# Linear attention and MLP on one Trainium2 core: the second product spread over two loops, token block 2 in row form, batch 0 read as loaded

## The chip, the core and the metric

The kernel runs on one core of a Trainium2 chip. TensorE (PE, with its weight loads listed as PEld), VectorE (DVE), ScalarE (ACT), GpSimd (POOL) and SyncE (SP) each work through their own instructions in order and wait for one another through semaphores; 16 DMA engines move data for the queues of POOL, SP and ACT. The metric is the device time of one execution in microseconds (us), the median of several.

## The reference

Eight batches, eight heads, 576 tokens, 64 features per head. Inputs and output are float32.

```python
kv  = einsum('bhsd,bhse->bhde', k, v)          # 64 x 64 per batch and head
o   = einsum('bhsd,bhde->bhse', q, kv)
rms = sqrt(mean(o*o, axis=-1) + 1e-6)
x   = (o / rms * g_norm) -> [4608 tokens, 512]  # heads side by side
h   = x @ w_in                                  # 512 -> 2048
g   = max(h, 0) + alpha * min(h, 0)             # alpha per feature
out = g @ w_out                                 # 2048 -> 512
```

## The kernel before

**Blocks.** The 4608 tokens are cut into nine blocks `w` of 512. A batch has 576 tokens, so a block holds tokens of one or two batches. All matmul operands are fp16; sums are fp32 in PSUM.

**Loads.** POOL's queue loads q, k and v of a batch and casts them to fp16. The first 512 tokens go into staging tiles (`qst`, `kst`, `vst`, L167), the last 64 into `qsb`, `ksb`, `vsb` (`load_rem`, L185). For batches 0 to 2 a partition holds several neighbouring tokens, so the output rows are stored in a permuted grid (`row_pieces`, L552). v is read by TensorE from where it was loaded. k, and q of the early batches, are first copied into an order by token (`regroup0` L215 for batch 0, `regroup` L191, in pairs on ACT from batch 3 on), and TensorE reads the copies.

**Attention in column form (blocks 0 to 2).** For each pair of heads `j`: `step_t` turns q with TensorE transposes (L327), and ACT or DVE copies the result to `qt_sb`; `step_kv` (L371) multiplies k by v for both heads at once, 128x128, and DVE keeps the two diagonal quarters by a mask (L379); `step_ot` (L393) gives o with features on partitions, 128x512; ACT squares it (L400), a matmul with a mask of ones adds the squares over the 64 features (`ssq_ps`, L416), ACT makes the reciprocal root (L420), and DVE writes `xt` (L429), the moving operand of the first product.

**Attention in row form (blocks 3 to 8, `W_ROW = 3`).** q is turned by DMA transposes on SP's queue (`dma_t`, L356). `row_kv` (L994) makes the 64x64 product of each head, and ACT copies them into `kv_masked`. `rows_mm` (L439) gives o with tokens on partitions, four tiles of 128 tokens. For each tile ACT squares 128x512 in one instruction (`rows_sq`, L463), DVE adds the squares with one reduction (`rows_ssq`, L469), ACT makes the reciprocal root of 128x8 (L479), DVE multiplies (`rows_norm`, L487), and a DMA transpose on SP's queue brings the tile into `xt` (L492).

**First product.** For each of 16 groups `g` of 128 of the 2048 features, four matmuls of 512 columns fill one PSUM bank (`m1_mm`, L507). ACT writes relu(-h) to `m_sb` (L514), and DVE writes `gt` = (1 - alpha) * relu(-h) + h (L518). From block 2 on two banks take turns for this (`h1`, `h2`; `h_bank`, L500), so group u + 2 can't begin before the `gt` of group u is written. From block 3 on the group at the head of a loop is split (`m1_cols`, L528): three quarters of its columns first, the last quarter after a few other matmuls, when the last tile of `xt` has come.

**Second product.** Block 0 uses 64 plain matmuls of 512 columns (`y_mm`, L539). Blocks 1 to 8 use a form with seven half-size products, 16 matmuls of 256 columns each (`prod_mm`, L656): products 1 and 2 read `gt` alone and collect in bank X, 6, 7 and 4 in bank Y, 5 and 3 in bank Z. Products 6, 5, 7 and 3 read sums of `gt` parts that DVE makes (`s_sum`, L616: S2, S1, S3, S4), and all but 1, 2 and 3 read sums of `w_out` parts made once (`w_sum`, L592). DVE and ACT read the banks between products (`y_read`, L713) and POOL, SP or ACT store the rows.

**Order.** It is written out by hand. The early part (L805 to L960) lists block 0 and the attention of block 1 step by step. Then loop `w` from 1 to 8 (L1056) has 16 units `u`. A unit holds one group of the first product of block `w`, then seven matmuls of the second product of block `w - 1` (`PER`, `Y_LIST`; none in loop 1, whose units hold the last three plain matmuls of block 0 instead), then steps of the attention of block `w + 1` (`attention`, L1032, with the tables `ATT_1` and `ROW_AT`). Loads of batch `w + 2` are issued at the head of loop `w` (`load_gated`, L204). After loop 8 comes the second product of block 8. `g_norm` is applied to `xt` for blocks 0 to 2 and folded into `w_in` during loop 2 (`scale_w_in` on ACT, L246).

Of the kernel before, what the change touches and what calls it, by code (L numbers as in the profile page):

```python
# [9 lines left out]
FP32 = mybir.dt.float32  # L10
# [7 lines left out]
def kernel(  # L18
# [32 lines left out]
    W_ROW = 3  # L51
# [81 lines left out]

    alpha_row = ysb_p.tile([P, D_MODEL], FP32, name="y_sb")
# [11 lines left out]
    for i in range(NBUF):  # L146
        t = {}
        for nm in ("k", "v", "q") if i < 2 else ("k", "v"):
            n = 1 if nm == "v" else T0 if i == 0 else NT
            t[nm] = qkv_p.tile([P, n, H, D], FP16, name=f"{nm}sb{i}")  # L150
            if i > 0 or nm == "v":
                nc.vector.memset(t[nm][REM:P, n - 1, :, :], 0.0)
        bufs.append(t)
    stages = {}

    def load0(nm, j, n=1):
        i, h = divmod(2 * j, HH)
        if (0, nm, i) not in stages:
            stages[0, nm, i] = stage_p.tile([P, HH, T0, D], FP16, name=f"{nm}st", tag=f"{nm}st")
# [5 lines left out]
    def load_main(b, nm, h0=0, h1=H):  # L165
        if (b, nm) not in stages:
            stages[b, nm] = stage_p.tile([P, H, TPP, D], FP16, name=f"{nm}st", tag=f"{nm}st")  # L167
# [5 lines left out]
    def load_q(b):  # L173
        st = stage_p.tile([P, TPP, H, D], FP16, name="qst", tag="qst")
# [7 lines left out]
    def buf_of(b, nm):  # L182
        return bufs[min(b, B_NAT) % 2 if nm == "q" else b % NBUF][nm]

    def load_rem(b, nm):  # L185
        nc.gpsimd.dma_start(
            out=buf_of(b, nm)[0:REM, 0 if nm == "v" else TPP, :, :],
# [16 lines left out]
    def load_gated(b):  # L204
        load_rem(b, "q")
        if b == B_NAT:
            load_q(b)
        load_rem(b, "k")
        load_main(b, "k")
        if b > B_NAT:  # L210
            load_q(b)
        load_rem(b, "v")
        load_main(b, "v")

# [6 lines left out]

    def regroup_pair(b, nm, j):
        regroup(b, nm, 2 * j, 2 * j + 2, nc.scalar)

# [17 lines left out]
    def scale_w_in(g):  # L242
        i = max(n for n, f0 in enumerate(IN_CUTS[:-1]) if f0 <= g * P)
        f0 = g * P - IN_CUTS[i]
        blk = w_in_sb[i][:, :, f0 : f0 + P]
        nc.scalar.activation(out=blk, in_=blk, func=AF.Copy, scale=g2col[:])  # L246

    def load_w_out(i):
        t = w_p.tile([P, GW, D_MODEL], FP16, name=f"w_out_sb{i}")
        for r in range(0, GW, GW // 2):  # L250
            g = i * GW + r
            nc.gpsimd.dma_start(
                out=t[:, r : r + GW // 2, :],
                in_=moe_w_out[g * P : (g + GW // 2) * P, :].rearrange("(g p) m -> p g m", p=P),
            )
        w_out_sb.append(t)
# [20 lines left out]
    for i in range(len(IN_CUTS) - 1):  # L277
        load_w_in(i)
    load_batch(1, ("k",))
    load_w_out(0)  # L280
    load_main(1, "q")
    load_w_out(1)
# [3 lines left out]
    load_w_out(2)  # L286
    load_w_out(3)
    load_rem(1, "q")

# [13 lines left out]
    kv_masked = [const_p.tile([P, NPAIR, P], FP16, name=f"kv_masked{i}") for i in range(2)]  # L303
# [20 lines left out]
    def transposes(qt_ps, c, b, j, ts):  # L324
        n = rows(b)
        for t in ts:
# [29 lines left out]
    def dma_t(b, ts=tuple(range(NT))):  # L356
        qt = qt_sb[b % 2][:, :, PAD : PAD + S]
        for t in ts:
            c0, c1 = t * P, min((t + 1) * P, S)
            src = stages[b, "q"][:, t] if t < TPP else buf_of(b, "q")[0:REM, TPP]  # L360
# [5 lines left out]

    def step_kv(b, j, pool=(ps_s, "s")):
        ks, vs = pair_cols(b, "k", j), pair_cols(b, "v", j)
# [9 lines left out]
        kvs[b, j] = kv_masked[b % 2][:, j, :]  # L378
# [5 lines left out]
    def step_ot(w, j, pool=None, parts=1):  # L384
# [13 lines left out]
        sq = attn_p.tile([P, W], FP16, name="sq_sb")  # L398
# [27 lines left out]
    def norm(w, j, parts=1):  # L426
        ot_ps, rstd = ots.pop((w, j))
        for c in col_parts(parts):
            nc.vector.scalar_tensor_tensor(  # L429
# [9 lines left out]
    def rows_mm(w, i0):  # L439
        o_ps = row_tile([2, 2, NPAIR, D], "or_ps")  # L440
        for i in (i0 + 1, i0):
            b, r = divmod(w * W + i * P, S)
            for j in range(NPAIR):
# [5 lines left out]
                for n, (bb, c) in enumerate(steps):  # L449
                    for h in range(2):  # L450
                        part = slice(h * D, (h + 1) * D)
                        nc.tensor.matmul(  # L452
                            out=o_ps[:, h, i - i0, j, :],
# [4 lines left out]
            ots[w, "r", i] = o_ps[:, :, i - i0]  # L458

    def rows_sq(w, i):  # L460
        o_ps = ots.pop((w, "r", i))
        sq = attn_p.tile([P, 2, NPAIR, D], FP16, name="sq_sb")
        nc.scalar.activation(out=sq[:], in_=o_ps, func=AF.Square)  # L463
        ots[w, "r", i] = (o_ps, sq)

    def rows_ssq(w, i):
        o_ps, sq = ots.pop((w, "r", i))
        ssq = attn_p.tile([P, 2, NPAIR], FP32, name="ssq_r")
        nc.vector.tensor_reduce(  # L469
            out=ssq[:].rearrange("p h j -> p (h j)"),  # L470
            in_=sq[:].rearrange("p h j d -> p (h j) d"),
            axis=mybir.AxisListType.X, op=ALU.add,
        )
        ots[w, "r", i] = (o_ps, ssq)

    def rows_rs(w, i):
        o_ps, ssq = ots.pop((w, "r", i))
        rstd = attn_p.tile([P, 2, NPAIR], FP32, name="rstd_r")
# [5 lines left out]
    def rows_norm(w, i):  # L484
        o_ps, rstd = ots.pop((w, "r", i))
        xr = attn_p.tile([P, NPAIR, 2, D], FP16, name="x_rows", tag="rstd" if i % 2 else "x_rows")
# [9 lines left out]
    gts = {}  # L496
# [15 lines left out]
    def m1_evac(h_ps, w, g):  # L512
        m_sb = gt_p.tile([P, W], FP32, name="m_sb", bufs=2)
        nc.scalar.activation(out=m_sb[:], in_=h_ps[:], func=AF.Relu, scale=-1.0)  # L514
        i, r = divmod(g, 2)
        if (w, i) not in gts:
            gts[w, i] = gt_p.tile([P, 2, W], FP16, name="gt", tag=f"gt{i}")
        nc.vector.scalar_tensor_tensor(  # L518
            out=gts[w, i][:, r, :], in0=m_sb[:], scalar=beta_sb[:, g : g + 1], in1=h_ps[:],
            op0=ALU.mult, op1=ALU.add,  # L520
        )

# [14 lines left out]

    def y_mm(y, w, a, g):
        nc.tensor.matmul(  # L539
            out=y[:], lhsT=gt_cols(w, g, a * P, (a + 1) * P), rhs=w_out_blk(g),  # L540
            start=(g == 0), stop=(g == NF - 1),
# [3 lines left out]
    store_turn = [0]  # L545

# [28 lines left out]
    def y_out(y, w, a):  # L575
        y_sb = ysb_p.tile([P, D_MODEL], FP32, name="y_sb")
        nc.scalar.copy(out=y_sb[:], in_=y[:])
        store_rows(w * W + a * P, y_sb[:], 0, D_MODEL)
# [588 lines left out]
```

## Time and profile before

| | |
|---|---|
| median of three runs | 274.64 us (274.28 to 275.09) |
| profiled execution | 275.59 us, of which its span 273.6 us |
| granted TensorE clock, mean | 0.994 |
| PE busy | 266.3 us (97%), 2181 matmuls |
| DVE busy | 227.9 us (83%), 432 instructions |
| ACT busy | 155.9 us (57%), 294 instructions |
| POOL busy | 86.2 us (32%), 123 instructions |
| DMA | 34.56 MB in 87343 packets |

The busy times are shares of the span, which the hardware profiler recorded from the first to the last instruction. A matmul's duration in the profile includes its way through the array; the next one starts earlier, so the chain of work, which counts from start to start, gives the cost of a matmul in a dense stream: 0.86 us for four of 512 columns, 0.77 us for seven of 256. In a line of the chain the columns are the start in us, the length in us, and the work, merged over equal instructions. In a line of groups they are the source line, the engine and operation, output and input, the shape and the count, then the busy time in us and the mean duration of one in ns, then idle time before them and what ended it. In a line of the timeline they are the start and the length in us. In a line of stages they are the stretch in us, its length, then for PE, PEld, DVE, ACT and POOL the busy time (and count), then the granted clock, the DMA share and GB/s.

### The profile page before, as it was taken

To read this page: it belongs to the slowest core of one execution; us is meant where nothing else is said; L and a number is where in the kernel's file an instruction comes from. 1 tells how busy PE (TensorE), PEld (TensorE's weight loads), DVE (VectorE), ACT (ScalarE), POOL (GpSimd) and SP (SyncE) were. 2 spreads that over 40 slices of the span, in tenths; PEclk is the share of its full clock that TensorE was granted. 3 is DMA by queue.
4 is the path that set the end of the run, shared out by engine and by line. 5 is a ranking of instruction groups with operands and counts; after the bars stand their busy time and mean duration, and the time that the engine had idled before them with its cause. 6 is when DMAs were issued, how large, how long until landed. Compare 5 with 4: busy or idle time off the path is not lost.

```text
span 273.6 us, 5687 instructions
## 1 busy us (share of the span) xinstructions
PE 266.3 (97%) x2181; PEld 170.8 (62%) x2181; DVE 227.9 (83%) x432; ACT 155.9 (57%) x294; POOL 86.2 (32%) x123
## 2 busy tenths in 40 slices
PE   7799999999999999999999999999999999999995
PEld 2364464555666766666666666666666666666794
DVE  6459938899889979997999799979998999877863
ACT  3267555879989865645565556555544553443210
POOL 8773462780733355226421551100110012000200
PEclk9799999999999999999999999999999999999999
DMA  8999999999999689966996699720222122201223
GB/s 161 196 200 199 197 202 189 220 112 162 137 164 180 99 129 149 170 153 113 155 167 147 112 156 164 151 89 19 77 60 77 22 77 60 77 1 41 77 79 116
DMA packets 87343, 34.56 MB, mean 126 GB/s; under 512 B 58884, under 2 KB 85652, under 8 KB 87316
## 3 DMA queue, kind: packets, MB, share of 16 engines
q0 software_dynamic: 58064, 24.35, 69.5%
q1 hardware_dynamic: 28212, 8.83, 17.1%
q10 hardware_dynamic: 1040, 1.02, 1.2%
q8 instruction: 17, 0.28, 0.4%
q14 instruction: 10, 0.08, 0.1%
HBM read 36.71 MB, written 9.44 MB: 169 GB/s over the span
## 4 chain that ended last, share of the span: by engine, by line
PE 95%; DMA 2%; DVE 1%; issue 0%; ACT 0%; POOLq 0%
PE h_ps L507 43%; PE yY L688 15%; PE yX L688 10%; PE yZ L688 10%; PE y L539 5%; DMA vst<-in_v_dram 2%; PE h_ps L530 2%; PE kv_ps L371 2%; PE or_ps L452 1%; PE kv_ps L1001 1%; PE ssq_ps L416 1%; PE qt_ps L327 1%; PE ot_ps L393 1%; PE yZ L683 1%; PE warm_ps L295 0%
## 5 line engine op out<-in xcount | busy, mean ns | idle before, releaser
L507 PE MATMUL h_ps<-xt,w_in_sb 128*128 128x512 f16 x544 | 136.9, 379 | 0.0
L514 ACT ACTIVATE m_sb<-h_ps 128x512 f32<-128x512 f32 x144 | 86.1, 599 | 78.1 <-PE h_ps L507 67.7
L518 DVE SCALAR_TENSOR_TENSOR gt<-m_sb,beta_sb,h_ps 128x512 f16<-128x512 f32 x144 | 106.2, 744 | 24.1 <-ACT m_sb L514 22.5
L507 PEld LDWEIGHTS <-w_in_sb 128*128 128x128 f16 x544 | 52.1, 98 | 40.0
L550 POOL DMA_DIRECT2D out_dram<-y_sb x36 | 22.6, 630 | 134.3 <-ACT y_sb L726 53.4
L688 PEld LDWEIGHTS <-s 128*128 128x128 f16 x496 | 48.5, 98 | 19.1
L688 PEld LDWEIGHTS <-gt 128*128 128x128 f16 x384 | 37.3, 98 | 14.0
L688 PE MATMUL yY<-wsum,s 128*128 128x256 f16 x256 | 36.3, 273 | 0.0
L688 PE MATMUL yX<-w_out_sb,gt 128*128 128x256 f16 x256 | 36.1, 273 | 0.0
L177 POOL DMA_DIRECT2D qst<-in_q_dram x20 | 17.7, 923 | 1.8 <-DMA vst<-in_v_dram 1.8
L688 PE MATMUL yY<-wsum,gt 128*128 128x256 f16 x128 | 17.6, 273 | 0.0
L688 PE MATMUL yZ<-wsum,s 128*128 128x256 f16 x120 | 16.7, 273 | 0.0
L688 PE MATMUL yZ<-w_out_sb,s 128*128 128x256 f16 x120 | 16.7, 273 | 0.0
L487 DVE TENSOR_TENSOR x_rows<-or_ps,rstd_r 128x512 f16<-128x512 f32 x24 | 16.4, 683 | 0.0
L469 DVE TENSOR_REDUCE ssq_r<-sq_sb 128x8 f32<-128x512 f16 x24 | 16.3, 678 | 0.0
L463 ACT ACTIVATE sq_sb<-or_ps 128x512 f16<-128x512 f32 x24 | 14.4, 599 | 2.6 <-PE or_ps L452 2.6
L539 PE MATMUL y<-w_out_sb,gt 128*128 128x512 f16 x64 | 15.8, 379 | 0.0
L625 DVE TENSOR_TENSOR s<-s,gt 128x512 f16<-128x512 f16 x32 | 13.5, 421 | 0.5
L623 DVE TENSOR_TENSOR s<-gt 128x512 f16<-128x512 f16 x32 | 13.4, 418 | 0.0
L629 DVE TENSOR_TENSOR s<-gt,s 128x512 f16<-128x512 f16 x32 | 13.2, 417 | 0.0
L627 DVE TENSOR_TENSOR s<-gt 128x512 f16<-128x512 f16 x32 | 13.0, 418 | 0.0
L720 DVE TENSOR_TENSOR u<-yY,p 128x512 f32<-128x512 f32 x16 | 10.9, 683 | 1.9 <-PE yY L688 1.7
(88 smaller groups left out, 249.9 us busy)
## 6 DMA issues: line engine op xcount, KB each, us to landing
out_dram<-y_sb POOLq DMA_DIRECT2D x16, 256.0 KB, 2.7
kst<-in_k_dram POOLq DMA_DIRECT2D x7, 512.0 KB, 7.9
vst<-in_v_dram POOLq DMA_DIRECT2D x6, 512.0 KB, 10.5
qst<-in_q_dram POOLq DMA_DIRECT2D x20, 128.0 KB, 8.0
w_out_sb<-in_moe_w_out_dram POOLq DMA_DIRECT2D x8, 256.0 KB, 11.7
out_dram<-y_sb SPq DMA_DIRECT2D x5, 256.0 KB, 2.2
w_in_sb<-in_moe_w_in_dram POOLq DMA_DIRECT2D x2, 512.0 KB, 10.0
qst<-in_q_dram POOLq DMA_DIRECT2D x2, 512.0 KB, 12.1
```

What stands on the lines that cost most here:

```text
L177: nc.gpsimd.dma_start(out=st[:, t, :, :], in_=srcs["q"][b, :, t * P : (t + 1) * P, :].rearrange("h p d -> p h d"),)
L463: nc.scalar.activation(out=sq[:], in_=o_ps, func=AF.Square)
L469: nc.vector.tensor_reduce(out=ssq[:].rearrange("p h j -> p (h j)"), in_=sq[:].rearrange("p h j d -> p (h j) d"), axis=mybir.AxisListType.X ...
L487: nc.vector.tensor_tensor(out=xr[:].rearrange("p j h d -> p h j d"), in0=o_ps, in1=rstd[:].unsqueeze(3).to_broadcast([P, 2, NPAIR, D]), op ...
L507: nc.tensor.matmul(out=h_ps[:], lhsT=w_in_blk(c, g), rhs=xts[w][:, c, :], start=(c == 0), stop=(c == NC - 1),)
L514: nc.scalar.activation(out=m_sb[:], in_=h_ps[:], func=AF.Relu, scale=-1.0)
L518: nc.vector.scalar_tensor_tensor(out=gts[w, i][:, r, :], in0=m_sb[:], scalar=beta_sb[:, g : g + 1], in1=h_ps[:], op0=ALU.mult, op1=ALU.add,)
L539: nc.tensor.matmul(out=y[:], lhsT=gt_cols(w, g, a * P, (a + 1) * P), rhs=w_out_blk(g), start=(g == 0), stop=(g == NF - 1),)
L550: engs[store_turn[0] % len(engs)].dma_start(out=dst, in_=src)
L623: nc.vector.tensor_add(out=t[:], in0=a21, in1=a22)
L625: nc.vector.tensor_sub(out=t[:], in0=sums[w, 1, k][:], in1=a11)
L688: nc.tensor.matmul(out=bank, lhsT=lhs, rhs=rhs, start=fresh, stop=(c == NK - 1), skip_group_check=True,)
```

## The change

- **Second product over two loops.** Products 1 and 2 of block `w` (X, 32 matmuls) are spread over loop `w` itself and the first two units of loop `w + 1`; the other 80 (order 6, 7, 4, 5, 3) stay in loop `w + 1`. Tables give the number of matmuls per unit (`X_AT`, `YZ_AT`; 4 to 11 in all). Groups go in the order 0 to 15. X has bank `y`; Y and Z share bank `h0`. Where a Y or Z bank is read in a unit, the DVE half of that unit's group comes after the read (`behind`). The sums have one buffer each, at new places (`S_ALL` and others).
- **Block 2 in row form** (`W_ROW = 2`), its tiles 0 to 2 as rows; tile 3 is made in column form (`cols_mm`, `cols_sq`, `cols_rs`, `cols_norm`) and DVE writes it straight into `xt`. q of batch 2 is turned by DMA transposes.
- **Batch 0 read as loaded.** Transposes and k-v products of batch 0 read the staging tiles head by head (`cols0`, `step_kv0`), 64 columns of weights at a time; the seven-part `regroup0` is gone.
- **k of batches 2 to 7 read as loaded** (`head_rows`): no copies by DVE or ACT.
- **Squares of rows.** `rows_sq` makes the squares of a tile in eight ACT instructions of 128x64, each of which also adds its 64 squares (`accum_out`); the DVE reduction is left for the tiles marked `red` (in loops 3 to 6 one of four).
- **w_in scaled early**: on DVE and ACT during the second product of block 0 and in loop 1. For blocks 1 and up `xt` is then a plain product.
- **Loads**: the order of the `w_out` parts among the first loads is changed (`w_out` 0 ahead of the last `w_in` part). From loop 1 on k, q and v of batch `w + 2` are issued at separate units, most behind a small POOL copy that waits for a `gt` (`gate`). Three stores of block 0 are put off into loop 2 on SP's queue.
- After loop 8 the order of the products is another one (`LAST`).

```diff
-    W_ROW = 3
+    W_ROW = 2
...
+    def cols0(nm, j, i, t):
+        if nm != "v" and j == 0:
+            return bufs[0][nm][0:P0, t, i, :]
+        h = 2 * j % HH + i
+        return stages[0, nm, 2 * j // HH][0:P0, h, t, :]
+
+    def step_kv0(j, pool):
+        kv_ps = pool[0].tile([P, D], FP32, name="kv_ps", tag=pool[1])
+        for t in range(T0):
+            for i in range(2):
+                nc.tensor.matmul(
+                    out=kv_ps[i * D : (i + 1) * D, :], lhsT=cols0("k", j, i, t),
+                    rhs=cols0("v", j, i, t), start=(t == 0), stop=(t == T0 - 1),
+                    skip_group_check=True,
+                )
...
+    def cols_mm(w, i):
+        b, r = divmod(w * W + i * P, S)
+        t = row_tile([2, NPAIR, P], "oc_ps")
+        for j in range(NPAIR):
+            nc.tensor.matmul(
+                out=t[:, 0, j, :], lhsT=kvs[b, j], rhs=qts[b, j][:, r : r + P],
+                start=True, stop=True, skip_group_check=True,
+            )
+        ots[w, "c", i] = t
...
+    def cols_norm(w, i):
+        xt_cols(w, 0)
+        nc.vector.tensor_mul(
+            out=xts[w][:, :, i * P : (i + 1) * P], in0=ots.pop((w, "c", i))[:, 0],
+            in1=sqs.pop((w, i))[:].rearrange("p (j n) -> p j n", j=NPAIR),
+        )
...
+        if ROW_AT[w]["red"][i]:
+            if half == 0:
+                nc.scalar.activation(out=sq[:], in_=o_ps, func=AF.Square)
+            else:
+                nc.vector.tensor_reduce(...)
+            return
+        for j in range(NPAIR):
+            nc.scalar.activation(
+                out=sq[:, half, j], in_=o_ps[:, half, j], func=AF.Square,
+                accum_out=ssq[:, half, j : j + 1],
+            )
...
-    Y_ORDER = (1, 6, 2, 7, 5, 4, 3)
+    X_LIST, YZ_LIST = products(1, 2), products(6, 7, 4, 5, 3)
+    X_AT = [0, 0, 1, 3, 1, 0, 2, 3, 2, 3, 1, 0, 3, 1, 1, 7, 1, 3]
+    X_1 = [0, 0, 0, 0, 0, 0, 0, 0, 5, 0, 0, 1, 6, 4, 6, 8, 0, 2]
+    YZ_AT = [3, 6, 7, 5, 5, 6, 7, 3, 6, 8, 4, 4, 6, 5, 5, 0]
...
-    regroup0("q", 1)
-    regroup0("k", 1)
-    regroup0("q", 2, 2)
...
+    ROW_AT = {2: {'kv': 5, 'mm': {0: ((0,),), 7: ((1, 2), (3,))}, ...
+    for w in range(4, B):
+        ROW_AT[w] = {'kv': 3, 'mm': {4: ((1, 0), (3, 2))}, 'sq': (5, 5, 4, 6, 7, 7, 7, 8), 'rs': (6,
+            7, 8, 11), 'norm': (6, 9, 8, 11), 'red': (0, 0, 1, 0)}
+    COL_TILES = ((2, 3),)
...
+    for w in range(1, B - 2):
+        q, k, v = (1, 7, 12) if w == 1 else (2, 1, 11)
+        for nm, at in (("q", q), ("k", k), ("v", v)):
+            when = LOADS.setdefault((w + at // NF, at % NF), [])
+            if at > 1 or w == 1:
+                when.append(("gate", w, at - 1))
+            when.append((nm, w + 2))
...
+            if late:
+                m1_cols(h_ps, w, u, 0, W - P)
+            else:
+                m1_mm(h_ps, w, u, range(NC))
+                m1_neg(h_ps, w, u)
+                if not behind:
+                    m1_sum(h_ps, w, u)
+            unit_sums(w, u)
+            if u < 2 and w > 1:
+                x_prods(w - 1, NF + u)
+            x_prods(w, u)
+            if w > 1:
+                yz_prods(w - 1, u)
+            if behind:
+                m1_sum(h_ps, w, u)
```

In a row of squares, `'sq': (5, 5, 4, ...)` gives the unit of the first and second half of tile 0, then of tile 1, and so on; `'rs'` and `'norm'` give one unit per tile.

## The prediction

> **What bounds the kernel now.** I read the page's busy times and chain first, then the chain in the two stretches that the change rewrites, then the stages, then groups by shape and a piece of ACT's timeline.
>
> ```profile
> PE 266.3 (97%) x2181; PEld 170.8 (62%) x2181; DVE 227.9 (83%) x432; ACT 155.9 (57%) x294; POOL 86.2 (32%) x123
> PE 95%; DMA 2%; DVE 1%; issue 0%; ACT 0%; POOLq 0%
> ```
>
> TensorE bounds it, and the chain agrees with its busy time: nearly everything on it is matmuls issued back to back. So time can only come from matmuls removed, from the first 20 us, or be lost to a new wait of PE.
>
> ```profile
> 12.30 0.79 DVE qsb L217
> 13.09 0.55 DVE ksb L217
> 15.17 0.27 DVE ksb L217
> 51.12 0.28 PE qt_ps L327 x5
> 54.72 0.56 PE kv_ps L371 x10
> 57.56 0.44 PE ot_ps L393 x4
> 59.31 0.22 PE ssq_ps L416
> 71.80 0.75 PE kv_ps L1001 x40
> 72.56 0.97 PE h_ps L507 x4
> 74.29 0.69 PE or_ps L452 x40
> ```
>
> The chain, of 0 to 21 us and of 48 to 76 us. Early, three of the copies that the change drops stand on it. In loop 1 block 2's column form does. The last three lines price the row form: 40 small matmuls take 0.75 or 0.69, and the group behind them 0.97 instead of 0.86.
>
> ```profile
> 48.10:68.50 20.40, 20.39 (x134) 10.93 (x132) 18.13 (x33) 17.47 (x34) 10.51 (x15) 1.00 1.44 164
> 96.20:123.80 27.60, 27.60 (x255) 18.50 (x254) 24.76 (x46) 16.22 (x33) 10.48 (x14) 1.00 1.17 149
> ```
>
> Stages: loop 1, and a loop of row form. PE is full in both at full clock; DVE has little room, ACT much.
>
> ```profile
> L514 ACT ACTIVATE m_sb<-h_ps 128x512 f32<-128x512 f32 x144 | 86.1, 599 | 78.1 <-PE h_ps L507 67.7 <-PE h_ps L530 6.2 <-DVE gt L518 2.0
> L469 DVE TENSOR_REDUCE ssq_r<-sq_sb 128x8 f32<-128x512 f16 x24 | 16.3, 678 | 0.0
> L463 ACT ACTIVATE sq_sb<-or_ps 128x512 f16<-128x512 f32 x24 | 14.4, 599 | 2.6 <-PE or_ps L452 2.6
> L479 ACT ACTIVATE rstd_r<-ssq_r,eps_t 128x8 f32<-128x8 f32 x24 | 7.2, 298 | 0.6
> L400 ACT ACTIVATE sq_sb<-ot_ps 128x256 f16<-128x256 f32 x2 | 0.7, 382 | 0.0
> 16.97 0.66 ACT L400 ACTIVATE sq_sb<-ot_ps 128x256 f16<-128x256 f32 x2
> 102.46 0.59 ACT L463 ACTIVATE sq_sb<-or_ps 128x512 f16<-128x512 f32 x1
> 102.94 0.30 ACT L479 ACTIVATE rstd_r<-ssq_r,eps_t 128x8 f32<-128x8 f32 x1
> ```
>
> Groups, then the timeline. An ACT instruction starts about 0.1 before the last one ends: 0.48 from square to root, 0.28 between the two halves. I use such distances: ACT 0.50 for a 128x512 out of PSUM, 0.19 for a root; DVE likewise 0.66 for `gt`, 0.60 for reductions, norms and bank reads, 0.34 for sums.
>
> **The change part by part.**
>
> *Block 2.* Removed from PE in loop 1, all on the chain: 20 transposes, 0.28 + 0.28 + 0.30 + 0.44 = 1.30 with one stall of 0.18; 20 k-v matmuls, 2 x 0.56 = 1.12; o, 0.44 + 0.22 + 0.22 = 0.88; four `ssq_ps`, 0.22 + 0.22 + 0.25 + 0.23 = 0.92. Together 4.22. Added: the k-v run 0.75 + 0.11 = 0.86; 8 and 16 matmuls of `or_ps` at 0.69/40 less the entry, 0.32 and 0.44 with entry and exit (about 0.2) each; the column tile, four of 128 columns at 0.056 and one of 512, 0.44. Together 2.06. Gain 2.16. The head split of loop 2 costs PE 0.01. The five DMA transposes of q and three of `x_rows` go to SP's queue, whose transposes were out 2.3 to 7.8 us in the row loops; the q ones have loop 1 before them.
>
> *Batch 0.* `regroup0` takes 0.79 + 0.55 + 0.27 = 1.61 of chain. What is late next is loads and ACT: the last k and v parts are issued at 5.88 and 6.50 and land 7.3 and 7.4 later, at 13.9, against the last k-v group at 15.49; and the third o waits for ACT's copy of `qt_sb` behind a square. I take 1.2 of the 1.61 at the first dense matmuls. But the loads cap it: the `w_out` part issued at 28.98 lands 10.7 later, at 39.7, and the first `y` matmul that reads it ran at 40.42. Its place among the loads is not changed. So at most 0.75 survives, less the 0.22 of a `y` matmul put behind that point: I take 0.55, with 0 and 1.4 as ends.
>
> *Second product over two loops.* The same 112 matmuls of 256 columns in each loop, so nothing on PE. A unit holds 4 to 11 of them instead of 7. The tightest pair for `gt` is units 10 and 11: group 10's must be there 9 x 0.109 + 0.86 = 1.84 after its last matmul; ACT and DVE need 0.60 + 0.74 + about 0.1. Covered.
>
> *DVE and ACT in loop 1.* DVE: 16 `gt` 10.6, three reductions 1.8, four norms 2.4, four sums 1.3, four scalings of `w_in`. The scaling on DVE has no row: 0.34 (a sum of that shape) to 0.72 (the same work on ACT); I take 0.34, fp16 in and out like the sum. 17.5 in all, under PE's 19.8 (16 groups 13.8, 30 X matmuls 3.3, three `y` 0.65, attention 2.06). Covered, closely.
>
> *Steady loops.* DVE loses three reductions of four, and ACT the k copies. DVE: 22.0 of 27.6. ACT: 16 x 0.50 + two bank copies 0.93 + k-v copies 0.74 + one square 0.48 + four roots 0.77 = 10.9, and 24 small squares.
>
> *The small squares with their sum* (128x64) have no row. Low end: the line through 382 at 256 and 599 at 512 gives 0.22 at 64, less the overlap 0.10: 0.12. High end: 0.30, the root's whole duration, as if the sum's write let nothing overlap. I take 0.22, the same operation's line without overlap. Where it matters: units 4 to 8 of loops 3 to 6 give ACT 4, 8, 4, 4 and 4 of them, a full square and three roots. Counted from the end of group 5's matmuls, PE wants the banks of groups 6, 7, 8 and 9 at 4.03, 5.77, 7.83 and 9.24 (0.86 + 0.109 per product and unit). At 0.22 ACT ends `m_sb` of group 6 at 2.9, then 4.5, 6.6, 8.1; with DVE behind, `gt` is there at 3.7, 5.3, 7.3, 9.05. No wait, 0.2 to spare. From 0.24 on PE waits.
>
> *Stores and loads.* Not on the chain; the end after the last matmul (3.3 us) keeps its shape.
>
> Sum: 2.16 + 0.55 = 2.7. Against the profiled execution, 275.59 with a span of 273.6 and 2.0 around it: span 270.9, execution 272.9. That execution is 0.95 above the median of 274.64; from the median, **272.0**.
>
> **The rivals.**
>
> *A, slower: the small squares fill ACT's queue.* At 0.30 each the `gt` of groups 6 to 9 come 0.66, 0.25, 0.15 and 0.6 late, each after the wait before: 1.7 per loop. Loops 3 to 6, loop 2 with 32 of them, and half of it in loop 7, 5.5 x 1.7 = 9.3: **281**. It decides from 0.26, where the waits (3 us) use up the gain. For it: the write of a sum per instruction, which no row of before has. Against it: the overlap that ACT shows. The Trainium skill speaks for it: Advanced Engine Details and Errata, The Read-Write Bubble, says that the memory latency shows between instructions on ScalarE, and advises tiles of 512 or 1024 elements. The trace agrees in part: 382 against 599 for half the elements, but 0.1 of it overlapped. By that rule alone each would cost its whole 0.22, short of the turning point. Chance 0.20.
>
> *B: the last tile of `xt` meets the v load.* Its transpose now leaves about 2.65 after group 11's matmuls, as v's load starts. Alone such transposes took 2.4, under loads 4 to 7.8. The last quarter of group 0 wants it 7.6 after group 11. Landing is at 5 to 8.4, so up to 0.8 in each of loops 2 to 5: up to 3.2, **275**. Chance 0.09.
>
> *C, no gain: DVE bounds loop 1.* With scalings at 0.72 DVE has 19.0 of 19.8, its waits for tiles on top; then loop 1 keeps its length: **274.1**. Chance 0.08.
>
> **How the numbers follow.** The forecast has 0.60; 0.03 is left for other waits that slow it. The forecast's own range is 270.7 (1.4 at the start) to 273.5. The range for 8 in 10 goes from 270.6 to 275.6, which takes in B, C and small squares up to 0.265; it leaves out most of A. A difference under 0.3% (0.8 us) can't be told from none. Faster: the forecast, half of B and a part of C, 0.68; same 0.08; slower 0.24.
>
> **What would show it.** Right: small squares 0.12 to 0.24 apart; no wait of PE for `gt` in units 8 to 11; loop 1 some 2 us shorter without its X matmuls; last k-v of batch 0 near 14.1. Wrong: `m_sb` starting over a us after its matmuls from unit 6 on, with PE idle before `h_ps`; or PE idle before the last quarter of group 0 (B); or DVE without gaps in loop 1 (C).

## The result, and the profile after

The changed kernel took 281.03 us (median of 6 runs, 276.61 to 286.53), the kernel before 274.54 (6 runs, 274.11 to 275.09). The ratio is 1.0163, with a 95% interval of 1.0127 to 1.0199: slower by 1.6%, where 1% faster was forecast; by the medians it is 2.4%. The spread is part of the result: the kernel before stays within 1.0 us, the changed one spreads over 10, and its median is over all six runs, the ratio over its three faster ones (276.61, 280.04 and 280.31). The profiled execution took 280.04 with a span of 278.0 at full clock.

From page parts 1 and 4 of the changed kernel, busy times and the shares of the chain:

```profile
PE 265.8 (96%) x2250; PEld 168.6 (61%) x2250; DVE 218.0 (78%) x414; ACT 157.2 (57%) x547; POOL 86.2 (31%) x130
...
PE 61%; DMA 22%; issue 10%; POOL 2%; DVE 2%; SPq 2%; ACT 0%; POOLq 0%; ACTq 0%
```

PE is busy for about as long as before, but its share of the chain is 61% and that of DMAs 22%. In the profile that the prediction read, these were 95% and 2%. The kernel before, profiled once more (run 11 below), has this line on its page:

```profile
PE 87%; DMA 10%; POOL 1%; issue 1%; DVE 0%; POOLq 0%
```

So nearly half of the 22% is there without the change: it is loads of the first 33 us, and the rest is new. A share of the chain is not yet a loss, since it counts the whole of a DMA and not only the wait for it. The view of waits says which DMAs; it lists the engine and line that waited, what it waited for, then total us, times, and the longest:

```profile
PE h_ps L631 <- DMA xt<-x_rows: 2.2, 2, 1.6
PE oc_ps L512 <- DMA qt_sb<-qsb: 1.9, 1, 1.9
PE warm_ps L304 <- DVE y_sb L119: 1.5, 1, 1.5
PE or_ps L499 <- DMA qt_sb<-qst: 1.0, 2, 0.8
PE qt_ps L343 <- DVE qsb L209: 0.7, 1, 0.7
PE kv_ps L1129 <- DMA vst<-in_v_dram: 0.6, 1, 0.6
```

L631 is the first group of a loop, which needs the transposed tiles of `xt`; L512 is the column tile of block 2; L499 and L1129 are o and k-v in row form. From loop 1 on, all waits of this list are for DMAs, none for `gt`. In the view before, the same list had 1.2 on a DMA, at the very start, and no other.

To place the loss I cut each trace at the start of `m_sb` of the first group of each loop; a wait at the head of a loop so falls into the stretch of the loop before it. The last column is the end of the last matmul. "Before, again" is a second profile of the unchanged kernel, which the experiments explain; the last row is the best kernel of the experiments.

| | loop 0 starts | 0 | 1 | 2 | 3 | 4 | 5 | 6 | 7 | 8 | PE ends |
|---|---|---|---|---|---|---|---|---|---|---|---|
| before, as predicted from | 20.04 | 29.11 | 18.82 | 28.01 | 27.59 | 27.70 | 27.59 | 27.70 | 26.73 | 36.97 | 270.27 |
| before, again | 18.44 | 30.02 | 18.82 | 28.01 | 27.59 | 27.70 | 27.59 | 27.70 | 26.73 | 36.97 | 269.57 |
| changed | 18.15 | 30.36 | 22.88 | 29.03 | 27.59 | 29.45 | 27.59 | 28.04 | 27.71 | 34.18 | 274.98 |
| run with columns, last norm earlier | 18.87 | 29.81 | 20.40 | 28.08 | 27.59 | 27.70 | 27.59 | 27.70 | 26.73 | 34.18 | 268.64 |

Against "before, again" PE ends 5.41 later: 0.05 up to loop 1, +4.06 in loop 1, +1.02 in loop 2, +1.75 in loop 4, +0.34 in loop 6, +0.98 in loop 7, and -2.79 in loop 8, since every loop hands 30 X products to the loop before it and so, in sum, loop 8 to loop 1 (the second product over two loops). So loops 1 and 8 belong together: +1.27.

The single waits, read as the gap between two matmul starts beyond their usual distance: in loop 1, 0.12 behind a `gt`, 0.28 at the o tiles ahead of the column tile, and 2.09 at the column tile; 0.75 at the head of loop 2; in loop 2, 0.80 at the k-v product and 0.39 at the o tile of block 3; 1.76 at the head of loop 5, which is the stretch of loop 4; 0.34 in loop 6, of which 0.21 is for a `gt` and 0.13 behind DVE's read of a bank; 0.97 at the o tile in loop 7. Sum 7.5, and 7.0 of it for DMAs. Without the 3.24 of loop 1 and the head behind it, loops 1 and 8 would be 1.97 shorter than before.

The chain shows the pattern: first of loops 1 and 2, then of the end of loop 4, of the changed kernel (start, us, what):

```profile
52.05 6.83 DMA qt_sb<-qsb
58.88 0.05 issue
58.92 0.40 PE oc_ps L512 x4
...
67.36 6.49 DMA vst<-in_v_dram
73.85 6.89 DMA qt_sb<-qst
80.74 0.14 issue
80.88 0.41 PE or_ps L499 x16
```

```profile
149.24 0.60 DVE x_rows L580
...
149.87 7.13 DMA xt<-x_rows
157.00 0.04 issue
157.04 0.38 PE h_ps L631 x4
```

A transpose of a tile, which took 2.4 us where it ran alone, takes 6.8 to 7.1 here. In the first case q's loads of batch 3 were issued from 50.5 on, in the last v's load of batch 6 at 150.42, half a microsecond behind the transpose; it landed 10.1 later.

This row of page part 2 was there to be read before, too: the busy share of the DMA engines in 40 slices, first of the kernel before, then of the changed one.

```profile
DMA  8999999999999689966996699720222122201223
```

```profile
DMA  8999999997999999969996999496044213111123
```

One slice is 7 us. Up to about 85 us DMA has hardly any room in either kernel. The difference is what is due in that time.

ACT, which the largest rival had as the trouble, is not in the way. Its new instructions, from the timeline:

```profile
108.46 0.22 ACT L562 ACTIVATE sq_sb<-or_ps 128x64 f16<-128x64 f32 x1 [0.40 <-PE or_ps L499]
108.58 0.19 ACT L562 ACTIVATION_READ_ACCUMULATOR sq_sb<-or_ps 128x1 f32 x1
108.68 0.21 ACT L562 ACTIVATE sq_sb<-or_ps 128x64 f16<-128x64 f32 x1
108.78 0.20 ACT L562 ACTIVATION_READ_ACCUMULATOR sq_sb<-or_ps 128x1 f32 x1
```

A square with its sum is two instructions that start 0.10 apart: 0.20 for the pair, where 0.22 was taken and the turning point was 0.24.

### The profile page after: what moved, and what is told of

Same layout as the page of the kernel before. It is cut to its first block, busy times and chain, and to the rows that moved or that the text cites. A ratio compares the mean times of both kernels' runs of the same rounds, so it can differ in the third digit from the quotient of the medians.

```text
span 278.0 us, 6097 instructions
## 1 busy us (share of the span) xinstructions
PE 265.8 (96%) x2250; PEld 168.6 (61%) x2250; DVE 218.0 (78%) x414; ACT 157.2 (57%) x547; POOL 86.2 (31%) x130
## 3 DMA queue, kind: packets, MB, share of 16 engines
q10 hardware_dynamic: 1040, 1.02, 1.1%
## 4 chain that ended last, share of the span: by engine, by line
PE 61%; DMA 22%; issue 10%; POOL 2%; DVE 2%; SPq 2%; ACT 0%; POOLq 0%; ACTq 0%
PE h_ps L600 26%; PE yY L796 12%; DMA qst<-in_q_dram 7%; PE yZ L796 7%; PE yX L796 6%; PE y L643 4%; DMA qt_sb<-qst 3%; DMA w_in_sb<-in_moe_w_in_dram 3%; DMA xt<-x_rows 3%; DMA qt_sb<-qsb 2%; DMA vst<-in_v_dram 2%; SPq L380 2%; PE h_ps L631 1%; PE or_ps L499 1%; DMA out_dram<-y_sb 1%
## 5 line engine op out<-in xcount | busy, mean ns | idle before, releaser
L609 ACT ACTIVATE m_sb<-h_ps 128x512 f32<-128x512 f32 x144 | 88.1, 613 | 83.4 <-PE h_ps L600 64.7
L600 PEld LDWEIGHTS <-w_in_sb 128*128 128x128 f16 x540 | 51.3, 98 | 39.9 <-DMA w_in_sb<-in_moe_w_in_dram 0.6
L655 POOL DMA_DIRECT2D out_dram<-y_sb x32 | 20.5, 643 | 140.1 <-DVE y_sb L838 62.6
L796 PE MATMUL yX<-w_out_sb,gt 128*128 128x256 f16 x256 | 44.3, 273 | 0.0
L796 PE MATMUL yY<-wsum,s 128*128 128x256 f16 x256 | 35.2, 273 | 0.0
L562 ACT ACTIVATE sq_sb<-or_ps 128x64 f16<-128x64 f32 x152 | 33.1, 277 | 2.6 <-PE or_ps L499 2.6
L562 ACT ACTIVATION_READ_ACCUMULATOR sq_sb<-or_ps 128x1 f32 x152 | 32.6, 264 | 0.0
L580 DVE TENSOR_TENSOR x_rows<-or_ps,rstd_r 128x512 f16<-128x512 f32 x27 | 18.5, 687 | 1.0 <-ACT rstd_r L572 0.5
L796 PE MATMUL yY<-wsum,gt 128*128 128x256 f16 x128 | 17.6, 273 | 0.0
L796 PE MATMUL yZ<-wsum,s 128*128 128x256 f16 x120 | 17.5, 273 | 0.0
L731 DVE TENSOR_TENSOR s<-gt 128x512 f16<-128x512 f16 x32 | 12.9, 420 | 0.2
L735 DVE TENSOR_TENSOR s<-gt 128x512 f16<-128x512 f16 x32 | 12.3, 419 | 0.0
```

The costliest lines, as they stand in the source:

```text
L562: nc.scalar.activation(out=sq[:, half, j], in_=o_ps[:, half, j], func=AF.Square, accum_out=ssq[:, half, j : j + 1],)
L580: nc.vector.tensor_tensor(out=xr[:].rearrange("p j h d -> p h j d"), in0=o_ps, in1=rstd[:].unsqueeze(3).to_broadcast([P, 2, NPAIR, D]), op ...
L600: nc.tensor.matmul(out=h_ps[:], lhsT=w_in_blk(c, g), rhs=xts[w][:, c, :], start=(c == 0), stop=(c == NC - 1),)
L609: nc.scalar.activation(out=neg[w, g][:], in_=h_ps[:], func=AF.Relu, scale=-1.0)
L655: engs[store_turn[0] % len(engs)].dma_start(out=dst, in_=src)
L731: nc.vector.tensor_add(out=t[:], in0=a21, in1=a22)
```

## The experiments

Theory D: PE waits for DMAs, transposes above all, that run beside main loads. Theory A: the small squares fill ACT's queue (rival A of the prediction). Edits are against the changed kernel where nothing else is said.

**1. The v loads early.** `LOADS` only:

```
-        q, k, v = (1, 7, 12) if w == 1 else (2, 1, 11)
+        q, k, v = (1, 7, 12) if w == 1 else (2, 1, 3)
```

> The changed kernel with the v loads of loops 2 to 5 issued at unit 3 in place of unit 11. Theory D (PE waits for DMAs that meet loads): the 1.76 us before the last quarter of group 0 in loop 4 goes, and no such wait is left in loops 3 to 6; the waits of loop 1, of the head of loop 2 and of loop 7 stay. The profile's span falls from 278.0 to about 276.2, and the runs lie closer together, since that transpose came late in one loop of four only. Theory A (the small squares with their sum hold up gt): nothing changes, 278 again.

Measured: 280.15 (279.15 to 282.08), ratio 1.021 [1.016, 1.0259]; span 279.1. The wait at the head of loop 5 went (stretch of loop 4: 27.70), and no such wait is left from loop 3 on. But loop 2 grew to 32.29. The chain of this run there:

```profile
86.57 6.84 DMA out_dram<-y_sb
...
93.53 0.70 DVE y_sb L840
...
94.27 0.70 PE yZ L796 x5
```

The stores of block 0's y, which the change issues at unit 6 of loop 2, now met the v load; the buffer of `y_sb` came free at 93.41, DVE could not empty PE's bank before, and PE stood 2.2 us. The span is 279.1 where 276.2 was expected. The cure of the one place was right and made another of the same kind.

**2. Batch 3's loads later in loop 1.**

```
-        q, k, v = (1, 7, 12) if w == 1 else (2, 1, 11)
+        q, k, v = (5, 6, 7) if w == 1 else (2, 1, 11)
```

> The changed kernel with the loads of batch 3 in loop 1 issued at units 5, 6 and 7 in place of 1, 7 and 12 (q, k, v). Theory D: the three transposes of batch 2's q then run beside the rest of an older load only and land 2 us earlier, so the 2.09 before the column tile falls under 0.5; the head of loop 2 (0.75), the k-v product of block 3 (0.80) and its first o tile (0.39) lose most of theirs. Span about 278.0 - 3.5 = 274.5. Theory A: loop 1 keeps its 22.9 us, span 278.

Measured: 284.12 (282.01 to 286.23), ratio 1.0362 [1.0286, 1.0439]. The 2.09 before the column tile went altogether, and the 0.80 and 0.39 of loop 2 too, as expected. The head of loop 2 went the other way, from 0.75 to 6.2, and the span is 280.7 where 274.5 was expected. Chain of this run:

```profile
65.02 8.19 DMA xt<-x_rows
73.21 0.14 issue
73.35 1.86 PE h_ps L631 x8
```

The k and v loads, issued at 60.35 and 62.02, landed at 68.25 and 72.90; the transposes of `x_rows` left at 62.70 and 65.02 and landed at 72.62 and 73.21, with the v load. I had asked only what the loads left free, not what they would meet next.

**3. Both moves, and batch 7's q early.** Loads at (5, 6, 7) and (2, 1, 3), and in `QT_AT`

```
-        ... zip((13, 11, 13, 11, 9), rest)) ...
+        ... zip((0, 1, 2, 3, 4) if w == B - 1 else (13, 11, 13, 11, 9), rest)) ...
```

> Both load moves together, and the five transposes of batch 7's q issued at units 0 to 4 of loop 6 in place of 9 to 13. Theory D: all waits on DMAs from loop 1 on are gone, 2.09 + 0.28 + 0.75 + 0.80 + 0.39 + 1.76 + 0.97 = 7.0 of the span of 278.0, so 271 to 272.5, an execution of 273 to 274.5, below the kernel before by 0 to 1.5. Theory A: 278 less nothing.

Measured: 282.26 (280.62 to 282.49), ratio 1.0265 [1.0231, 1.03]. The head of loop 2 waits 6.8, where run 2 had 6.2; that wait is against the expectation, and with it the span of 280.7 in place of 271 to 272.5. From loop 3 on it holds: 27.59, 27.70, 27.59, 28.04, 26.73, with the stretches of loops 4 and 7 cured (29.45 and 27.71 before this edit).

**4. One square per row tile.** Every tile of `ROW_AT` with `'red': (1, 1, 1, 1)`, where the changed kernel has (0, 0, 0, 0) to (1, 1, 1, 0).

> The changed kernel with every row tile squared by one instruction of 512 columns and summed by a reduction on DVE, so that ACT has no small squares left. Theory A: the loss goes with them, span near 272. Theory D: the waits on DMAs stay, and the span stays within 1.5 of 278 (the DMA waits vary by as much), DVE 3 us per loop busier than the 22 it has now of 27.6.

Measured: 280.56 (279.57 to 280.91), ratio 1.021 [1.0183, 1.0238], span 277.5. Theory A is out: with no small square left the kernel is not faster, and the waits of the DMAs stay (1.7 for `qt_sb` at the column tile, 1.1 for v of batch 3, 0.2 for q of batch 3 and 0.8 for that of batch 7). A loop without such waits even takes 28.03 in place of 27.59, in two short gaps of PE (0.16 and 0.29, both for a `gt`) at the same place of every such loop: DVE, which has the reductions back, is late there.

**5. Block 2 in columns.** All four tiles as column tiles, so that loop 1 has no `x_rows` to transpose:

```
-    COL_TILES = ((2, 3),)
+    COL_TILES = ((2, 0), (2, 1), (2, 2), (2, 3))
-    ROW_AT = {2: {'kv': 5, 'mm': {0: ((0,),), 7: ((1, 2), (3,))}, ...
+    ROW_AT = {2: {'kv': 5, 'mm': {0: ((0,),), 7: ((1,), (2,)), 11: ((3,),)}, ...
```

with squares, roots and norms at units that fit.

> The changed kernel with all four tiles of block 2 in column form straight into xt, the last of them at unit 11, so that loop 1 has no transposes of x_rows and its third transpose of q is wanted at unit 11 in place of unit 7. Loads as in the changed kernel. Theory D (PE waits for DMAs that run beside loads): the waits of 2.09 and 0.28 in loop 1 and of 0.75 at the head of loop 2 go, three column tiles cost PE 0.6 more than three row tiles; the waits for v of batch 3 (0.80), for q of batch 3 (0.39) and the later ones stay. Loop 1 from 22.9 to about 20.3, span about 275.5. Theory E (the row form of block 2 is not at fault, its k-v product and DMA transposes of q are as late without x_rows): span 278.5.

Measured: 277.20 (275.87 to 281.49), ratio 1.0077 [1.0055, 1.0099]. The loss halves, and no wait is left at the head of loop 2. Loop 1 did not become shorter in the profile (23.02): 0.99 was still for q's transpose, under batch 3's loads as before, and 1.60 was of my making, the last tile waiting for its PSUM tile until the norm of an earlier one. The waits for v and q of batch 3 did not come: v's load was issued at 66.16 and landed at 73.17, where the changed kernel has 67.36 and 75.75, and loop 2 began no earlier than there. The profiled execution is the one of 281.49: the v load met the last transpose of loop 2, which landed after 8.07, and PE stood 2.7 at the head of loop 3.

**6. No main loads of batch 3.** In loop 1 a constant is written to its stages instead:

```
-                    load_main(x[0], what)
+                    nc.gpsimd.memset(stages[x[0], what][:], 0.25)
```

(for batch 3 alone, and for q likewise).

> The changed kernel without the three main loads of batch 3 in loop 1 (1.5 MB): its k, v and q tiles are filled with a constant on GpSimd, so the blocks that need batch 3 are not computed from their data. Everything else, the transposes and their order on SP's queue too, is as in the changed kernel. Theory D: the transposes of batch 2's q and of block 2's x_rows land in 2.4 to 4.6 us, in place of 4.6 to 6.8; the waits of 2.09, 0.75, 0.80 and 0.39 go, loop 1 takes about 20.2 and loop 2 about 27.8; span about 274. Theory F (SP's queue issues the transposes too late, whatever runs beside them): the 2.09 before the column tile and the 0.75 at the head of loop 2 stay, span 277.

Measured: 276.32 (275.37 to 283.72), ratio 1.005 [1.0031, 1.0068], span 274.4. The column tile waits no longer, and neither do k-v and o of block 3; the head of loop 2 has 0.47 left. The DMA view of 48 to 68 us gives the median from issue to landing; the changed kernel, then this run:

```profile
qt_sb<-qsb SPq DMA_TRANSPOSE x3, 5.8
xt<-x_rows SPq DMA_TRANSPOSE x3, 3.8
```

```profile
qt_sb<-qsb SPq DMA_TRANSPOSE x5, 4.6
xt<-x_rows SPq DMA_TRANSPOSE x3, 2.4
```

SP issued the transposes at the same distances from the loop's start; what changed is what ran beside them. Theory F is out. The run lost 1.7 in another place, ahead of the column tile, which I come back to under what was not expected; that delay does not explain the missing wait, for the third transpose of q landed 8.10 after the loop's start in place of 10.37, and the changed kernel wanted it at 8.29.

**7. All cures together.** Columns as in run 5, batch 7's q as in run 3, and

```
-        q, k, v = (1, 7, 12) if w == 1 else (2, 1, 11)
+        q, k, v = (5, 3, 4) if w == 1 else (2, 1, 11 if w == 2 else 3)
```

> All cures together: block 2 in column form (as in the run with all columns), the loads of batch 3 at units 3, 4 and 5 of loop 1 (k, v, q), the v loads of loops 3 to 5 at unit 3 and that of loop 2 where it was, and the five transposes of batch 7's q at units 0 to 4 of loop 6. Theory D: no wait of PE on a DMA above 0.4 from loop 1 on; loops 1 to 7 of 20.3, 27.9, 27.6, 27.7, 27.6, 28.0 and 26.7; span 270.8 to 272, an execution of 273 to 274, faster than the kernel before by 0.2 to 0.6%, and the runs within 0.3% of each other as those of the kernel before are, since no DMA is on the chain. Theory A (small squares on ACT): 277 or more.

Measured: 275.69 (12 runs, 274.90 to 279.31), ratio 1.0054 [1.0025, 1.0082], span 273.5. No wait on a DMA is left from loop 1 on in the profile; the 1.60 for the PSUM tile is, and one v load (loop 2) is still beside a transpose. The runs still spread over 4.4, and the median is 0.5% slower than the kernel before where 0.2 to 0.6% faster was expected.

**8 and 9. That load and that wait out of the way.** Last column tile at unit 12; v of batch 4 at unit 4; the stores of block 0's y at unit 3 of loop 2:

```
-    LOADS.setdefault((2, 6), [])[0:0] = (("put", 0), ("put", 2), ("put", 1))
+    LOADS.setdefault((2, 3), [])[0:0] = (("put", 0), ("put", 2), ("put", 1))
```

> The run with all cures, with two waits more taken out of the way: the last column tile of block 2 at unit 12 in place of 11 (it stood 1.60 us for its PSUM tile), and in loop 2 the stores of y of block 0 at unit 3 in place of 6 and the v load of batch 4 at unit 4 in place of 11, so that no main load of loops 2 to 5 is under way when the last tile of xt is transposed. Theory D: span 273.5 - 1.6 = 271.9, an execution of about 273.7, faster than the kernel before by 0.2 to 0.5%; and the runs lie within 1.5 us of each other, where those of the run with all cures lie 4.4 apart, because the only transpose that could still come late is gone. If the scatter has another cause than late DMAs (the clock, the start), it stays at 4 us.

Measured: 274.24 (the others from 273.88 to 275.22; one execution, the profiled one, ran with every engine six times slower and is left out, trace and all); ratio 0.9991 [0.9976, 1.0006]. The spread is gone, as expected for late DMAs. Of the 1.6 about 1 came: the next two traces, of the same loop 1, show 0.71 at the head of loop 2, now for DVE's norm of the last tile.

Run 9 also swaps the main loads of batch 1's k and q in loop 0:

> The run before, with the main load of batch 1's q ahead of that of k in loop 0. Theory: the 0.83 that PE stands before the first transposes of batch 1 is the q load's landing at 32.6 (it was at 32.63 in the kernel before, too), so it goes when q lands at 28, and k in its place is wanted only at 38: span 0.5 to 0.8 shorter than without this edit. If k's copies on DVE hold up the scaling of the weights instead, nothing is gained.

Measured: 274.47 (274.00 to 275.07), ratio 0.9997 [0.9984, 1.0011]. Nothing gained: the wait for q went, but 0.52 came at a `y` matmul and 0.97 at k-v, for a `w_out` part and v.

**10. Batch 0's copies put back,** on the kernel of run 8: the five `regroup0` calls again, and the matmuls of 64 columns read the copies.

> The run with the stores at unit 3, with the copies of batch 0's q and k put back on DVE (five regroup copies), the matmuls reading the copies; the matmuls are the same. Theory: the first h_ps matmul of loop 0 starts 1.2 to 1.9 us later, but the waits of PE on loads in loop 0 (0.2 + 0.83 + 0.3) shrink by 0.8 to 1.3, so the head of loop 1 and the end come only 0.3 to 0.7 later. If the start is worth its full price, the end comes 1.5 later.

Measured: 274.40 (274.00 to 275.88 without one execution as above), ratio 0.9996 [0.9979, 1.0014], against 0.9991 without the copies. Loop 0 starts at 17.91 with all five copies, where the kernels without them start at 17.6 to 18.9. The copies cost nothing that can be measured, which contradicts both ends of what I expected.

**11. The kernel before, once more,** unchanged.

> The kernel before, unchanged, profiled once more. In the profile that the prediction is summed on, PE stood 1.2 us for batch 0's first v (landed at 7.99) and the granted clock was 0.50 from 8.0 to 11.2. Theory G: that start was a late one, as that execution was 0.95 above the median; with v landing at 7.3 or before the clock stays at 1.0, the first m_sb starts near 18.5 to 19.2 in place of 20.04, and the span is about 272.7. If the start is a property of the kernel before, the half clock comes again and m_sb starts at 20.0.

Measured: 274.90, span 272.9. The stretch 8.0 to 11.2 us, in the first profile of the kernel before and in this one (length, then busy times of PE, PEld, DVE, ACT, POOL, then the granted clock, DMA and GB/s):

```profile
8.00:11.20 3.20, 3.17 (x17) 1.55 (x16) 0.98 (x4) 0.60 (x2) 2.17 (x3) 0.50 1.31 199
```

```profile
8.00:11.20 3.20, 2.67 (x20) 1.15 (x21) 1.91 (x6) 1.34 (x3) 2.09 (x4) 1.00 1.28 190
```

In the first, v had landed at 7.99, PE had stood 1.2, and its clock was at half for 3 us. In the second v landed at 7.12, and the clock stayed full: loop 0 starts at 18.44 in place of 20.04. The start that I meant to shorten was that one execution's. Its chain there was so, too. These are the three longest pieces of the chain of the second profile up to 33 us:

```profile
3.95 6.45 DMA qst<-in_q_dram
10.69 6.71 DMA w_in_sb<-in_moe_w_in_dram
17.68 14.89 DMA qst<-in_q_dram
```

None of the copies is on it: there the kernel before follows its loads.

**12. The batch 0 part alone, on the kernel before:** `cols0`, `step_kv0` and the transposes of 64 columns from the change, no `regroup0`.

> The kernel before with the batch 0 part alone: its q and k read as loaded, 64 columns a matmul, no regroup copies. As predicted (the copies are worth 1.2 at the start, the loads cap it): 0.5 faster, 274.0. Theory G (the copies were waiting for loads and clock, not the other way): the same within 0.3, 274.5.

Measured: 274.54 (273.91 to 275.03), ratio 0.9999 [0.9987, 1.0011]. The part is worth nothing. Loop 1 starts at 48.55, against 48.46 in run 11.

**13. Columns, with the last norm one unit earlier** (root at 13, norm at 14), else run 8.

> The kernel with the loads freed and block 2 in columns, with the last tile's root and norm one unit earlier (13 and 14). Theory D: the 0.71 at the head of loop 2, where the last quarter of group 0 waited for that norm, goes: 273.6 where that kernel had 274.3; faster than the kernel before by 0.3%. If DVE is the bound there, the norm only trades places with gt and 274.3 stays.

Measured: 273.55 (273.13 to 274.06), ratio 0.9958 [0.9942, 0.9975]: faster than the kernel before by 0.4%, and the best of all. What is left in its view of waits:

```profile
PE kv_ps L396 <- DMA vst<-in_v_dram: 1.6, 2, 1.0
PE warm_ps L304 <- DVE y_sb L119: 1.5, 1, 1.5
PE qt_ps L343 <- DVE qsb L209: 0.3, 1, 0.3
```

All three lie before 33 us, the first two before the dense work begins.

**14. The same loads, block 2 in rows again:** run 8's loads and stores, `ROW_AT` and `COL_TILES` of the changed kernel.

> The same loads and stores as in that kernel, with block 2 as the changed kernel has it: three row tiles and their transposes of x_rows, one column tile at unit 7. It differs from that kernel by the form of block 2 alone. Theory D: PE's work is 0.6 less, but the transposes of x_rows leave at 62 to 65, under the loads of batch 3 that end at 70, and the head of loop 2 waits for them 3 to 5 us: 277 to 279. If the row form is not at fault, 273.5.

Measured: 279.45 (279.04 to 280.67), ratio 1.0183 [1.0159, 1.0206]. Its chain and two stretches of it:

```profile
64.44 7.49 DMA xt<-x_rows
71.93 0.14 issue
72.07 1.86 PE h_ps L631 x8
```

```profile
67.50:72.00 4.50, 0.28 (x3) 0.00 (x1) 2.09 (x5) 0.05 (x1) 0.00 (x0) 0.96 1.67 161
72.00:74.90 2.90, 2.83 (x11) 1.45 (x12) 0.30 (x1) 0.60 (x1) 0.00 (x0) 0.50 0.91 196
```

PE stands 4.4 for the transpose, and then runs 2.9 at half clock. Between runs 14 and 8 only block 2's form and its units differ: 279.45 against 274.24, 5.2 us (ratios to the kernel before 1.0183 and 0.9991), though in rows PE has about 0.8 less to do (loops 1 and 8 together are 1.97 shorter than before without their waits, in columns 1.21). So with loads that hurt nothing else, the row form of block 2 is what costs: its transposes are due at the head of loop 2, and batch 3's loads, wanted soon after, are under way until 72.

## Why the prediction was wrong

**Block 2's matmuls: right.** Forecast 2.16 less on PE; loops 1 and 8 together, less their waits, are 1.97 shorter. The mechanism and its size held, and by run 13, in columns, 1.21 of it can be had. Without the 7.5 of waits PE would end 2.1 ahead of the kernel before, an estimate from the table.

**Where it failed: "The five DMA transposes of q and three of `x_rows` go to SP's queue ... the q ones have loop 1 before them", and "Stores and loads. Not on the chain".** I quoted 2.3 to 7.8 for such transposes, the right range, and did not put either end against a due time. The third transpose of q is issued at 52.05 and wanted at 56.8, 4.75 later; at 2.4 it is in time, at 6.83 it is 2.1 late. Nor did I ask where the loads had gone: the change moves them from the loop's head to units 1, 7 and 12, or 2, 1 and 11, into the stretches where the transposes now fall due. Runs 2, 6, 13 and 14 show the cause by its removal and its return. That cost 3.12 up to the head of loop 2, 1.19 in loop 2, 1.76 at the head of loop 5 and 0.97 in loop 7.

**Rival B: the right mechanism, in one place of four and too small.** It gave up to 0.8 in each of loops 2 to 5. In the one trace it was 1.76 at the head of loop 5 and nothing at the others; in runs 2, 4, 5 and 6, with the same v loads, 1.6, 0.5, 2.7 and 1.1 at one head of loops 3 to 6 each. Part of the size was lost in its own sum: a transpose that leaves at 2.65 and takes 4 to 7.8 under loads lands at 6.7 to 10.5 and not "at 5 to 8.4", so by its own rows it could be up to 2.9 late, not 0.8; the one at the head of loop 5 took 7.13. It had a chance of 0.09 because I held it to the last tile of `xt`; the same clash of a transpose with a load stood at four other places. Whether the transpose or the load wins is not fixed from run to run, which fits the spread of 10 us: it is 4.4 in run 7 with one such v load left, and 0.9 in run 13 with none. Between those runs three things were changed, so that this one load is the cause is likely and not shown.

**Batch 0: wrong, and hidden by another error.** "`regroup0` takes 0.79 + 0.55 + 0.27 = 1.61 of chain": on the chain they were, but of an execution that was late because of its v load and a half clock. Runs 10 and 12 put the worth of the copies at zero within 0.3. In the second profile the chain does not pass through the copies, and of the 1.60 by which loop 0 starts earlier there, 0.70 is left at the last matmul. So the reading that time can be had from the first 20 us held for one execution; in the other, loads bound the kernel up to 33 us. A step on the chain is worth its time only if what stands beside it, the loads here, is not due at the same moment. The forecast had an execution 0.95 above the median before its eyes and did not ask which 0.95.

**Second product over two loops, DVE in loop 1: right.** Loops 3 and 5 take 27.59, as before. The scaling of `w_in` on DVE takes 0.35, where 0.34 was taken; rival C did not happen.

**Small squares: near at 0.22** (0.20 measured), though by another way: 0.22 was one instruction without overlap, and the trace has two that overlap, 0.10 apart. That the two sizes meet is luck. No wait for `gt` came in units 8 to 11 of the steady loops. Rival A named 281 and the time came out at 281.03; that is chance, for run 4 has no small squares and is no faster.

Of the signs that were announced, PE idle before the last quarter of group 0 came, and a loop 1 shorter by 2 us could be seen only after its waits were taken off. The last k-v of batch 0, announced near 14.1, starts at 13.61, but the kernel before in its second profile already has it at 14.18. The gaps of 0.34 in loop 6 came and went between runs 3, 5, 7 and 10. In the changed kernel DVE began the `gt` that PE waited for 0.45 after its `m_sb` was done, in run 14 0.09 after; why is open.

## What to carry to other kernels

A DMA that is added or moved needs three times: when it is issued, when it is wanted, and how long it takes beside the loads that the same change puts next to it; if the slack lies between its time alone and its time under loads, count it as late. Read the DMA row of the page as you read PE's: where it is full, moving a load can only move the wait, as in runs 1 and 2, and it must be moved past something that has slack. And before pricing a start, look at the granted clock of that stretch and at a second profile of the kernel.

## What was not expected of the hardware

- **A transpose beside loads takes about twice as long, and up to four times.** Alone 2.3 to 2.4; over these runs, eight of ten that overlap a load of q, k or v take 3.1 to 8.0, with a median of 5.1 and a longest of 10.2. Three of ten land within 0.7 of such a load (run 2: 72.62 and 73.21, the v load 72.90). The Trainium skill, DMA: Bandwidth & Descriptors, Queues, rings and completion order, says that each DMA engine goes round the queue rows it has work for, packet by packet; the traces agree with sharing, by the times above. No run here shows the order of packets.
- **The clock drops after short waits.** After waits of 2.2 (run 1), 2.7 (run 5) and 4.4 (run 14) PE was granted 0.50 for 3.41 us, and with those of 6.2 (run 2) and 6.8 (run 3) for 6.83, a part of it within the wait; after 2.09 and 1.76 in the changed kernel it kept 1.00. At the start of the kernel before, after warm-up matmuls, 1.2 was enough. The Trainium skill, TensorE: Matmul & The Clock Gate, What's actually happening, gives an idle window of about 3.4 us; the runs show shorter waits to be enough. An added wait from about 2 us on can so cost more than itself: in run 14 PE ran 2.9 us at half clock behind it, which is 1.5 us lost.
- **A memset on GpSimd held up DVE, seen once.** In run 6, from the timelines of DVE and POOL:

```profile
49.17 0.35 DVE L245 TENSOR_SCALAR w_in_sb<-w_in_sb,g2col 128x512 f16<-128x512 f16 x1
...
50.51 1.96 DVE L245 TENSOR_SCALAR w_in_sb<-w_in_sb,g2col 128x512 f16<-128x512 f16 x1
```

```profile
50.49 1.82 POOL L1250 MEMSET qst<- 128x2048 f16 x1
```

The same scaling took 0.35 and, beside the memset, 1.96; PE waited 1.6 for the `gt` behind it. The run's other two memsets stood beside other work of DVE, which kept its time (a reduction 0.68, a `gt` 0.74). So run 6 without this would have been near 272.7 of span, an estimate from its 274.4.
